# A gated mix of linear attention and a GeGLU feed-forward: tile 0's key sums ahead of the q folds, an up result copied by another engine, and other banks for the q folds

## The chip, the cores and the metric

The kernel runs on one core of one Trainium2 chip. The metric is the device time of one execution in microseconds (us). The core has a matrix engine (TensorE, PE in the profile; its weight loads are shown apart as PEld), a vector engine (VectorE, DVE), an engine for activations (ScalarE, ACT), GpSimd (POOL) and SyncE (SP), which here only issues DMAs. Each engine works through its own queue in order and waits on semaphores that other engines raise. TensorE writes its results into PSUM, which the kernel uses as eight banks of 512 float32 columns, numbered 0 to 7. A bank has to be emptied by VectorE or ScalarE before TensorE may write it again.

## What is computed

```python
# x: 2048 tokens x 640; 32 heads of 20; feed-forward width 1728
g = sigmoid((x * gate_w).sum(-1, keepdims=True))
q, k, v = split(x @ wqkv)                      # each 2048 x 32 x 20
pq, pk = q @ w_phi[h], k @ w_phi[h]            # per head, 20 x 20
phi_q = concat(softmax(pq), softmax(-pq))      # 40 features per head
phi_k = concat(softmax(pk), softmax(-pk))
kv  = sum_s phi_k[s] (outer) v[s];  z = sum_s phi_k[s]
a = ((phi_q @ kv) / (phi_q @ z + 1e-6)) @ wo
b = (gelu_tanh(x @ w_gate) * (x @ w_up)) @ w_down
out = g * a + (1 - g) * b
```

## The kernel before

The 2048 tokens are 16 tiles of 128 (the feed-forward works on 4 blocks of 512). `attention_state` writes out by hand the order in which work is issued to the engines, and a small scheduler (`_Sched`) turns each read and write of a buffer or a bank into semaphore waits. There is no planner: what a line issues goes to the end of its engine's queue.

Four steps matter here.

**Folding.** The per-head 20 x 20 matrix is multiplied into the key weights and the query weights ahead of the tiles: `fold("k", ...)` and `fold("q", ...)`, 55 small matmuls each (L400). The results fill five banks with a row block each (the `main` list, one bank for each of the five blocks `kt` = 0 to 4) and two banks with the remaining heads (the `tail` list). The softmax does not change when one of its 20 columns is subtracted from the others, so only 19 columns are kept: `fold_evac` copies the reference column (L426 on ScalarE, L428 on VectorE for block 0) and subtracts it on VectorE (L429). Block 3 goes another way: `fold_stage` copies the whole bank to SBUF on ScalarE (L438), and GpSimd subtracts (L442). `evacs` is the order in which VectorE empties the banks. A "strip" in that list (L449) is a memset of 19 columns of the second bank of a pair, which pads the last group of three heads.

**Key, value and query tiles.** `k_tile`, `v_tile` and `q_tile` take a pair of banks (b, b+1) and run ten matmuls of some 304 to 345 columns (L452), five for each bank. ScalarE then takes two exponentials from the pair (L523), for tiles 0 to 3 and 5 a small gate exponential as well (L513), or copies the values (L493). A query tile's exponentials leave through a DMA transpose on SP (L561). `k_norm(t)` is `k_sums(t)` (a VectorE sum over each head's features, L574) and `k_scale(t)` (a reciprocal, L582, and a multiplication, L583). `gram(t)` multiplies the normalised keys with the values (L594). The loop over the 16 tiles issues 12 more key tiles, the query tiles, 7 value tiles and 12 grams.

**Up results ahead of time.** `up_ahead(j, b, ek)` computes one chunk of `x @ w_up` for the first 512 tokens into bank b and copies it to SBUF, on VectorE (L538) or ScalarE (L541). Chunks 4, 5 and 6 are made early (`upf`), chunks 2 and 3 late (`upl`), just before the q folds. The feed-forward then runs only the gate half of these chunks for block 0.

**Feed-forward.** `gateups(0)` runs the chunks in the order 0, 1, 13, 2, 3, and so on, on the bank pairs (0,1) and (6,7) in turn. Chunk 13 is half as wide: one bank, a half-height gelu (L728) and two half products on VectorE (L733). Other chunks have a gelu (L720) and one product (L722). The last four grams are issued behind chunks 0, 1, 13 and 2. Chunk 3 writes bank 0, which chunk 13 used.

The order written out around the change is:

```python
v(6, 2); v(7, 4); k(0, 6)
up_ahead(3, ...); up_ahead(4, ...)
fold("q", ...)
k(1, 2); k(2, 4); k(3, 0); v(8, 6)
k_norm(0); k_norm(1); k_norm(2); k_norm(3)
for s in range(16): ...
```

Of the kernel before, what the change touches and what calls it, by code (L numbers as in the profile page):

```python
# [3 lines left out]
P = 128  # L4
BF16 = mybir.dt.bfloat16
F32 = mybir.dt.float32
AF = mybir.ActivationFunctionType
# [100 lines left out]
class _Kernel:  # L108
# [269 lines left out]
        i = s // 2  # L378
        return kt, i, (a - self.HLO[i]) * self.DH, c * self.DH, (z - a + 1) * self.DH

    def fold(self, name, main, tail, evacs):

        sc = self.sc
        wT, wkey = (self.wkT, "wkT") if name == "k" else (self.wqT, "wqT")
        M = lambda r, kt: (main[kt], [self.fold_item(r, kt, s, False) for s in range(r, 8, 2)])
        T = lambda r, j: (tail[j], [self.fold_item(r, kt, s, True) for kt in ((0, 1, 2), (3, 4))[j]
                                    for s in ((8,), (7, 9))[r]])
        halves = ([M(0, 0), M(0, 1), M(0, 2), T(0, 1), M(0, 3), M(0, 4), T(0, 0)],
                  [M(1, 3), M(1, 4), T(1, 0), M(1, 0), M(1, 1), M(1, 2), T(1, 1)])
        order = []  # L390
        for r, runs in enumerate(halves):
            at = 0
            for b, items in runs:
                for x, it in enumerate(items):
                    order.append((at, r, b, x == 0, x == len(items) - 1, it))
                    at += it[-1]
        opener = {}
        for _, r, b, top, bot, (kt, i, k0, c, n) in sorted(order, key=lambda o: o[:2]):
            a, opens = 64 * r, opener.setdefault(b, r) == r
            sc.op("pe", lambda e: e.matmul(  # L400
                self.bank(b)[:, c:c + n], wT[a:a + 64, i, kt * P:(kt + 1) * P],
                self.BD[a:a + 64, i, k0:k0 + n], start=opens and top, stop=bot and not opens, skip_group_check=True),
                reads=[wkey, ("BD", i)], writes=[("ps", b)] + ([("turn", b)] if bot else []), signal=bot,
                after=[("turn", b)] if top and not opens else ())
        self.fold_stage(name, 3, main[3])
        for what, x in evacs:
            if what == "strip":
                self.strip(x)
            elif what == "tail":
                self.fold_evac(name, (0, 3)[x], (3, 2)[x], tail[x], self.HM, self.H)  # L410
            else:
                self.fold_evac(name, x, 1, main[x], 0, self.HM)
# [30 lines left out]
            dst, src[:, :, 0:self.E], src[:, :, self.E].unsqueeze(2).to_broadcast([P, self.HM, self.E]), ALU.subtract),  # L443
            reads=[key], writes=[("w%s2" % name, kt)])

    def strip(self, b):

        c = (b + 1) * 512 + 304
        self.sc.op("dve", lambda e: e.memset(self.ps[:, c:c + self.E], 0.0), writes=[("ps", b + 1)])  # L449

    def mm(self, bank, c0, n, lhs, rhs, first, fin, reads):
        self.sc.op("pe", lambda e: e.matmul(  # L452
# [174 lines left out]
    def attention_state(self):  # L627
        NT = self.NT
        sc = self.sc
        ones = self.nc.const_aps.tensor(1.0, [P, 512], BF16)  # L630
        for n in (512, 512, 512, 512, 512, 512, 128, 128, 128):
            sc.op("pe", lambda e: e.matmul(self.bank(0, n), ones[:, 0:P], ones[:, 0:n], start=True, stop=True),  # L632
                  writes=[("ps", 0)])
        vs, ve, xt = self.v_step, self.v_first_evac, self.x_transpose
        xt(0, "d")
        xt(1, "a")
        for i in range(3):
            for a, b in ((0, 2), (64, 3)):
                sc.op("pe", lambda e: e.matmul(self.bank(b, P), ones[a:a + 64, 0:P], ones[a:a + 64, 0:P], start=True,
                                               stop=True), writes=[("ps", b)])  # L640
        xt(2, "d")
        xt(3, "a")
        for kt in range(4):
            for t in range(4):
                vs(t, kt)
        self.blockdiag()
        self.gate_column(6)
        for t in range(4):
            vs(t, 4)
            ve([t], "ad"[t % 2], False)  # L650
            if t == 2:
                ve([0, 1, 2], "a", True)
        ve([3], "d", True)
        v, k, q = self.v_tile, self.k_tile, self.q_tile
        self.up_ahead(0, 7, "d")
        self.up_ahead(1, 6, "a")
        self.up_ahead(2, 4, "d")
        v(4, 2)
        self.v_split(5, 0)
        m, t, p = "main", "tail", "strip"  # L660
        self.fold("k", (3, 4, 6, 5, 7), (0, 1), [(m, 0), (m, 1), (m, 2), (m, 4), (p, 6), (t, 0), (t, 1)])
        v(6, 2)
        v(7, 4)
        k(0, 6)
        self.up_ahead(3, 3, "d")
        self.up_ahead(4, 2, "a")
        self.fold("q", (3, 4, 5, 0, 1), (6, 7), [(m, 0), (p, 2), (m, 1), (m, 2), (p, 4), (m, 4), (p, 0), (t, 0), (t, 1),
                                               (p, 6)])
        k(1, 2)
        k(2, 4)  # L670
        k(3, 0)
        v(8, 6)
        self.k_norm(0)
        for t in range(1, 4):
            self.k_norm(t)
        nk, nv, ng = 4, 9, 0
        pieces = self.gate_pieces()
        for s in range(NT):
            r = s % 4
            if r != 1:  # L680
                k(nk, 2)
                self.k_norm(nk)
                nk += 1
            if s and r != 0:
                self.gram(ng)
                ng += 1
            if s and r in (0, 1):
                v(nv, 0)
                nv += 1
            q(s, 6)  # L690
            if s:
                pieces.pop(0)()
        for p in pieces:
            p()
        self.down_weights()
# [244 lines left out]
```

## Time and profile before

| | |
|---|---|
| Median of 3 runs | 284.63 us (284.04 to 284.73) |
| The profiled execution's own time | 284.38 us |
| Its span, first to last instruction | 283.1 us |
| Granted TensorE clock | 1.000 |
| PE busy | 278.9 us (98%) |
| PEld busy | 173.5 us (61%) |
| DVE busy | 173.7 us (61%) |
| ACT busy | 106.8 us (38%) |
| POOL busy | 15.1 us (5%) |

The profile is of one execution. "Busy" is the union of an engine's instructions on the time axis. A matmul's row runs from its start to its modelled end, and the next one starts before that end, so what TensorE loses is read from the starts of successive groups and not from its busy share. A bracket such as [0.30 <-DVE ps L449] behind a row gives the idle time of the engine just before that instruction and what ended it, as it is inferred from semaphore events.

### The profile page before, as it was taken

The numbers are of one execution on the slowest core, as the hardware profiler recorded it, in microseconds if no ns is written. First come the engines' busy times: TensorE is split into PE (matmuls) and PEld (weight loads), VectorE is DVE, ScalarE is ACT, GpSimd is POOL, SyncE is SP. The second block draws the span as 40 slices with busy tenths as digits, with TensorE's granted clock in tenths as the row PEclk, the third lists the DMA queues.
The fourth block names the chain that finished last, engine by engine and source line by source line (L and its number), as shares of the span: only waits on it lengthen the run. The fifth ranks groups of instructions, "written<-read, shape, count | busy, mean of one in ns | idle before, by whom it ended". The sixth has DMA issues, their size and how long they took to land.

```text
span 283.1 us, 6982 instructions
## 1 busy us (share of the span) xinstructions
PE 278.9 (98%) x2958; PEld 173.5 (61%) x2972; DVE 173.7 (61%) x329; ACT 106.8 (38%) x201; POOL 15.1 (5%) x69
## 2 busy tenths in 40 slices
PE   8999999999999999999999999999999999999996
PEld 4566777777765444444444444445777777777786
DVE  1365999999999523667243324225883883883801
ACT  4246987878783423223232223221112112112011
POOL 7511010101100000000000000000000000000000
DMA  7999079888799920011000000000152152242221
GB/s 229 211 214 187 4 132 151 165 162 162 147 187 244 347 81 2 0 23 27 0 0 0 2 0 0 2 0 0 25 77 63 53 63 60 71 52 68 73 72 49
DMA packets 60234, 24.11 MB, mean 85 GB/s; under 512 B 50986, under 2 KB 59690, under 8 KB 60202
## 3 DMA queue, kind: packets, MB, share of 16 engines
q1 hardware_dynamic: 59536, 23.63, 39.5%
q8 instruction: 23, 0.38, 0.6%
q10 hardware_dynamic: 666, 0.03, 0.2%
q14 instruction: 9, 0.07, 0.1%
HBM read 9.04 MB, written 2.62 MB: 41 GB/s over the span
## 4 chain that ended last, share of the span: by engine, by line
PE 76%; DVE 13%; issue 9%; ACT 0%; DVEq 0%; ACTq 0%
PE ps L452 41%; PE ps L804 29%; DVE Dk L574 9%; DVE Dk L582 3%; PE ps L464 2%; PE ps L749 2%; PE ps L632 1%; PE ps L400 1%; DVE wq L429 0%; PE ps L341 0%; DVE hT L722 0%; DVE Ek L583 0%; ACT gl L720 0%; DVE hT L733 0%; ACT outsb L817 0%
## 5 line engine op out<-in xcount | busy, mean ns | idle before, releaser
L452 PE MATMUL ps<-xT,wu_sb 128*128 128x512 bf16 x255 | 63.0, 379 | 0.4
L452 PE MATMUL ps<-xT,wg_sb 128*128 128x512 bf16 x251 | 62.0, 379 | 0.9 <-ACT gl L720 0.3
L720 ACT ACTIVATE gl<-ps 128x512 bf16<-128x512 f32 x52 | 31.0, 597 | 71.0 <-PE ps L452 68.0
L804 PE MATMUL ps<-wd_sb,hT 64*128 64x320 bf16 x648 | 48.4, 296 | 0.0
L722 DVE TENSOR_TENSOR hT<-ps,gl 128x512 bf16<-128x512 f32 x34 | 23.2, 690 | 37.7 <-PE ps L452 37.7
L452 PEld LDWEIGHTS ps<-xT,wu_sb 128*128 128x128 bf16 x260 | 25.4, 98 | 30.4
L452 PEld LDWEIGHTS ps<-xT,wg_sb 128*128 128x128 bf16 x260 | 25.0, 98 | 29.8 <-issue 0.6
L817 ACT ACTIVATE outsb<-ps,Gm 128x320 bf16<-128x320 f32 (+2 forms) x31 | 14.5, 515 | 71.8 <-PE ps L804 71.8
L452 PE MATMUL ps<-w,xT 128*128 128x304 bf16 (+5 forms) x280 | 40.3, 296 | 0.0
L804 PEld LDWEIGHTS ps<-wd_sb,hT 64*128 64x128 bf16 x648 | 30.9, 94 | 12.2 <-issue 0.4
L452 PEld LDWEIGHTS ps<-w,xT 128*128 128x128 bf16 x280 | 26.2, 97 | 10.8 <-DVE ps L449 0.3
L804 PE MATMUL ps<-wo_sb,goT 64*128 64x320 bf16 (+2 forms) x340 | 26.5, 288 | 0.0
L583 DVE TENSOR_TENSOR Ek<-Ek,Dk 128x1320 bf16<-128x1320 bf16 x16 | 24.5, 1533 | 0.5
L775 DVE TENSOR_TENSOR O<-ps,RH 128x640 bf16<-128x640 f32 x32 | 24.8, 815 | 0.0
L574 DVE TENSOR_REDUCE Dk<-Ek 128x66 f32<-128x1320 bf16 x16 | 24.3, 1519 | 0.1
L452 PE MATMUL ps<-wq,xT 128*128 128x304 bf16 x160 | 23.3, 292 | 0.0
L523 ACT ACTIVATE Eqt<-ps 128x627 bf16<-128x627 f32 x32 | 20.5, 693 | 6.4 <-PE ps L452 6.4
L523 ACT ACTIVATE Ek<-ps 128x627 bf16<-128x627 f32 x32 | 20.5, 693 | 2.3 <-PE ps L452 2.0
L722 DVE TENSOR_TENSOR xT<-ps,gl 128x512 bf16<-128x512 f32 x13 | 9.0, 692 | 18.2 <-PE ps L452 18.2
L804 PEld LDWEIGHTS ps<-wo_sb,goT 64*128 64x128 bf16 x340 | 15.9, 94 | 5.3
L452 PEld LDWEIGHTS ps<-wq,xT 128*128 128x128 bf16 x160 | 15.0, 97 | 4.5
L804 PE MATMUL ps<-wd_sb,xT 64*128 64x320 bf16 (+2 forms) x270 | 16.0, 269 | 0.0
(89 smaller groups left out, 186.0 us busy)
## 6 DMA issues: line engine op xcount, KB each, us to landing
out_dram<-outsb SPq DMA_DIRECT2D x7, 320.0 KB, 2.4
wd_sb<-in_B_w_down_dram SPq DMA_DIRECT2D x1, 2080.0 KB, 10.2
wg_sb<-in_B_w_gate_dram SPq DMA_DIRECT2D x5, 224.0 KB, 3.6
wg_sb<-in_B_w_gate_dram SPq DMA_DIRECT2D x5, 192.0 KB, 3.7
wu_sb<-in_B_w_up_dram SPq DMA_DIRECT2D x5, 192.0 KB, 5.0
w<-in_A_wqkv_dram SPq DMA_DIRECT2D x5, 160.0 KB, 3.9
wo_sb<-in_A_wo_dram SPq DMA_DIRECT2D x1, 800.0 KB, 9.7
xtok<-in_A_x_dram SPq DMA_DIRECT2D x2, 320.0 KB, 3.1
```

Of the source, the lines that this page charges most:

```text
L452: self.sc.op("pe", lambda e: e.matmul(self.ps[:, bank * 512 + c0:bank * 512 + c0 + n], lhs, rhs, start=first, stop=fin), reads=reads, writ ...
L464: sc.op("pe", lambda e, c0=c0, n=n, bk=bk, col=col: e.matmul(self.bank(bk)[:, col:col + n], self.xT[:, kt, t * P:(t + 1) * P], self.w3[:, ...
L523: self.sc.op("act", lambda e: e.activation(dst, src, AF.Exp, scale=scale), reads=[("ps", b), ("ps", b + 1)], writes=[(name, sl, s)])
L574: self.sc.op("dve", lambda e: e.tensor_reduce(self.Dk[:, se, 0, :].rearrange("p (u h) -> p u h", h=self.HG), self.k_view(se), AX.X, ALU.ad ...
L582: sc.op("dve", lambda e: e.reciprocal(R, D), reads=[("Dk", se)], writes=[("Rk", se)])
L583: sc.op("dve", lambda e: e.tensor_tensor(v, v, R.rearrange("p (u h) -> p u h", h=self.HG).unsqueeze(3).to_broadcast([P, 2 * self.G, self.H ...
L720: sc.op("act", lambda e: e.activation(self.gl[:, slot, :], self.bank(banks[0]), AF.Gelu_apprx_tanh), reads=[("ps", banks[0])], writes=[("g ...
L722: sc.op("dve", lambda e: e.tensor_tensor(hT, up, self.gl[:, slot, :], ALU.mult), reads=[upk, ("gl", slot)], writes=[("hT", hk, c)], guard=old)
L749: sc.op("pe", lambda e: e.matmul(self.ps[:, o:o + n], self.Eq[a:a + 64, g, t * P:(t + 1) * P], self.KV[a:a + 64, g, 0:n], start=(g in (0, ...
L775: dve(lambda e, o=o, f=f, s=s: e.tensor_tensor(o, V[s][:, :, 0:DH], f, ALU.mult), rb + [key(6 + s)], [("O", s, sl)], guard=old)
L804: sc.op("pe", lambda e: e.matmul(self.bank(bk, w), lhs, rhs, start=opens and x == 0, stop=end and not opens, skip_group_check=True), reads ...
L817: sc.op("act", lambda e: e.activation(dst, self.bank(bk, w), AF.Copy, scale=g), reads=rd, writes=wr)
```

## The change

```diff
-    def fold(self, name, main, tail, evacs):
+    def fold(self, name, main, tail, evacs, clear=None):
...
         self.fold_stage(name, 3, main[3])
+        if clear is not None:
+            self.strip(clear, "a")
         for what, x in evacs:
...
-    def strip(self, b):
+    def strip(self, b, ek="d"):
         c = (b + 1) * 512 + 304
-        self.sc.op("dve", lambda e: e.memset(self.ps[:, c:c + self.E], 0.0), writes=[("ps", b + 1)])
+        dst, wr = self.ps[:, c:c + self.E], [("ps", b + 1)]
+        if ek == "d":
+            self.sc.op("dve", lambda e: e.memset(dst, 0.0), writes=wr)
+        else:
+            zero = self.nc.const_aps.tensor(0.0, [P, self.E], F32)
+            self.sc.op("act", lambda e: e.activation(dst, zero, AF.Copy), writes=wr)
...
-        self.up_ahead(3, 3, "d")
+        self.up_ahead(3, 0, "a")
         self.up_ahead(4, 2, "a")
-        self.fold("q", (3, 4, 5, 0, 1), (6, 7), [(m, 0), (p, 2), (m, 1), (m, 2), (p, 4), (m, 4), (p, 0), (t, 0), (t, 1),
-                                               (p, 6)])
+        self.k_sums(0)
+        self.fold("q", (4, 5, 0, 3, 1), (6, 7), [(m, 0), (m, 1), (p, 4), (m, 2), (m, 4), (p, 0), (t, 0), (t, 1), (p, 6)],
+                  2)
         k(1, 2)
         k(2, 4)
         k(3, 0)
         v(8, 6)
-        self.k_norm(0)
+        self.k_scale(0)
         for t in range(1, 4):
             self.k_norm(t)
```

The late up result of chunk 2 goes to bank 0 instead of bank 3, and ScalarE copies it out instead of VectorE. VectorE's sum for key tile 0 is issued ahead of the q folds' evacuation instead of behind it. The row blocks 0 to 4 of the q fold go to banks 4, 5, 0, 3, 1 instead of 3, 4, 5, 0, 1, so the block that ScalarE stages now lies in bank 3. The strip of bank 3 is written by ScalarE, right behind that staging, instead of by a VectorE memset behind block 0. TensorE's instructions are the same in number and order, and only banks differ. No DMA is added, removed or moved.

## The prediction

> **What bounds the kernel now.** I read the chain of waits first, then the windows, then the timeline around the two places that the change touches. In the chain (start, length, work) VectorE's key sums seem to hold everything from 29.6 to 87.3 us:
>
> ```profile
> 29.61 1.51 DVE Dk L574
> 31.15 0.58 DVE Dk L582
> ...
> 87.27 0.96 DVE hT L722 x2
> 88.58 0.44 DVE hT L733
> 89.02 0.59 ACT gl L720
> 89.62 7.50 PE ps L452 x34
> ```
>
> The windows qualify that (columns: length; busy PE, PEld, DVE, ACT, POOL, each with its count; clock; DMA share; GB/s):
>
> ```profile
> 25.90:32.67 6.77, 6.77 (x54) 4.66 (x51) 6.42 (x13) 5.53 (x17) 0.98 (x1) 1.00 0.39 85
> 32.67:81.29 48.62, 48.62 (x474) 36.88 (x472) 47.73 (x41) 39.98 (x69) 4.31 (x11) 1.00 0.81 148
> 81.29:89.62 8.33, 7.90 (x75) 4.36 (x75) 7.98 (x10) 4.94 (x7) 0.00 (x0) 1.00 1.02 229
> ```
>
> In the long middle VectorE is busy for 47.73 of 48.62 us, but so is TensorE, and the clock is full. What TensorE loses has to be counted from starts. In the timeline a query or key tile takes 1.29 us from its start to the next group's (35.67 to 36.96), a value tile 1.36 (34.31 to 35.67), a gram 0.35 (33.96 to 34.31), ten 512-column matmuls 2.15 (83.81 to 85.96), five of them 1.07 (86.31 to 87.38).
>
> - 25.90 to 32.67: four key tiles and one value tile, 4 x 1.29 + 1.36 = 6.52 of 6.77. Lost: about 0.25.
> - 32.67 to 81.29: 16 query tiles, 11 key tiles, 7 value tiles, 12 grams: 27 x 1.29 + 7 x 1.36 + 12 x 0.35 = 48.55 of 48.62. Lost: under 0.1.
> - 81.29 to 89.62: 2 x 2.15 + 2 x 1.07 + 4 x 0.35 = 7.84 of 8.33. Lost: 0.49, nearly all behind the last gram, which starts at 88.80 and should hand over at 89.15; chunk 3 starts at 89.62, 0.47 late.
>
> So TensorE bounds the kernel, and VectorE's backlog reaches it at two spots only. The first, in the timeline (start, length, engine, line, operation, idle time before):
>
> ```profile
> 23.84 0.69 DVE L538 COPY upl<-ps 128x512 f32<-128x512 f32 x1 [1.96 <-PE ps L452]
> 23.98 0.18 ACT L513 ACTIVATE gcol<-ps 128x1 f32<-128x1 f32 x1
> 24.91 0.60 ACT L541 ACTIVATE upl<-ps 128x512 f32<-128x512 f32 x1 [0.76 <-PE ps L452]
> 25.62 0.18 DVE L428 COPY wref<-ps 128x25 f32<-128x25 f32 x1 [1.09 <-PE ps L400]
> 25.69 0.59 ACT L438 ACTIVATE qstage<-ps 128x500 f32<-128x500 f32 x1 [0.18 <-PE ps L400]
> 26.57 0.07 DVE L449 MEMSET ps<- 128x19 f32 x1
> 26.70 0.37 PEld L452 LDWEIGHTS ps<-w,xT 128*128 128x128 bf16 x4 [0.30 <-DVE ps L449]
> 29.61 1.50 DVE L574 TENSOR_REDUCE Dk<-Ek 128x66 f32<-128x1320 bf16 x1
> ```
>
> Tile 1's keys start at 25.90 in bank 2; their second half is due at 25.90 + 0.65 = 26.55 but starts at 26.70, when VectorE's strip has cleared bank 3. The second spot, with a later chunk 13 as the undisturbed case below the dots:
>
> ```profile
> 87.58 0.59 ACT L728 ACTIVATE gl<-ps 64x512 bf16<-64x512 f32 x1 [1.90 <-PE ps L452]
> 88.58 0.89 DVE L733 TENSOR_TENSOR hT<-ps,gl 64x256 bf16<-64x256 f32 x2
> 89.59 4.01 PEld L452 LDWEIGHTS ps<-xT,wg_sb 128*128 128x128 bf16 x20 [0.41 <-issue]
> ...
> 112.48 0.59 ACT L728 ACTIVATE gl<-ps 64x512 bf16<-64x512 f32 x1 [1.56 <-PE ps L452]
> 113.17 0.89 DVE L733 TENSOR_TENSOR hT<-ps,gl 64x256 bf16<-64x256 f32 x2 [1.08 <-ACT gl L728]
> ```
>
> Chunk 3 needs bank 0, whose last readers are chunk 13's two products. They start 1.00 us after their gelu's start here and 0.69 later on, because VectorE is behind. They end at 88.58 + 0.89 = 89.47, and chunk 3 loads its weights 0.12 later. After 89.62 TensorE goes on to the end, so what it gains by then stays gained.
>
> **The change part by part.**
>
> *The up copy.* VectorE loses a 0.69 us copy, ScalarE gains one of 0.60 (its row at 24.91). ScalarE is free after its gate exponential at 24.16, so the copy lies at 24.16 to 24.76, in the 0.76 us that it idled; the second copy stays at 24.91. The fold reaches bank 0 in its third run, a quarter or so into 1.08 us that begin at 24.81: about 25.1. The cover is 0.3 us; without it each further microsecond delays the fold. Cost: nothing.
>
> *The sums of tile 0.* Their input is ready at 24.10 (exponentials at 22.82 plus 1.28). VectorE, which idled from the end of its copy at 24.53 to 25.62, runs 1.50 us from about 24.17 to 25.67. Behind it in the queue stands the whole evacuation of the fold, which starts at 25.70 instead of 25.62: 0.08 late. Five q evacuations feed banks 4, 5, 0, 1, 6 and 7 to the key and value tiles that TensorE issues next.
>
> *Strip and banks.* One 0.07 memset leaves VectorE. The ScalarE strip has no row: the gate exponential (0.17 to 0.18, one column) and the reference copies (five, median 0.21) bound it at 0.17 to 0.21. It waits for the staging copy of the same bank, which ends at 25.69 + 0.59 = 26.28; so it ends at 26.50 to 26.55, and TensorE's second half starts at 26.55 to 26.60 instead of 26.70. The reference copies behind it slip some 0.2, so block 1's subtraction starts at about 26.68 instead of at the end of block 0's (26.58), 0.1 late. Then, at 0.65 a block and 0.45 a tail: bank 4 free at 26.6 (due 27.2), bank 5 at 27.4 (due 27.85), bank 0 at 28.05 (due 28.5), bank 1 at 28.8 (due 29.15), bank 6 at 29.25 (due 29.8). Smallest slack 0.35. Gain of TensorE here: s = 0.12, between 0 (a strip as late as VectorE's) and 0.25 (all that is lost in this stretch).
>
> One rule speaks against this part. The Trainium skill ("ScalarE: Activation LUTs", section "Rules for kernel authors") sends plain arithmetic to VectorE, and budgets about 0.3 us an ACTIVATE plus 0.83 ns an element; by it the strip would take an estimated 0.32 us, end at 26.65 and make s nothing. The one-column row at 0.18 says otherwise.
>
> *VectorE from there.* The evacuation ends at 29.7 and the sums are already done, so tile 1's sums start near 31.85 instead of 33.20. 1.35 us ahead (1.2 to 1.5), VectorE keeps that lead: its inputs are ready, closest for tile 14 (exponentials done at 78.27, sums at 80.06 before, 78.7 after). It ends the keys at 86.0 instead of 87.3.
>
> *The second spot.* Chunk 0's and 1's products then end at 87.3, before chunk 13's gelu does. The gelu starts at 87.58 - s; the products follow as in the later row, 0.69 + 0.89 = 1.58, and TensorE 0.12 + 0.03 behind them: 89.31 - s instead of 89.62. Gain 0.31 beside s; with the 0.05 step between a gate exponential's end at 39.85 and the weight load at 39.90, 0.38; at most 0.47, when TensorE is held by nothing; none, if the wait is another.
>
> The rest of VectorE's 1.35 us goes into idle time before chunk 13's products. A second rule would value it more: the Trainium skill ("Perfetto Trace Analysis", "Identifying the Most-Contended Engine") takes the engine with the highest occupancy as the one to speed up and distrusts TensorE's busy share. By occupancy the middle stretch is VectorE's, and the gain would be the whole 1.35 us. The count from starts leaves 0.1 us there.
>
> Sum: 0.12 + 0.31 = 0.43, with the shorter step 0.5; I take 0.45. The profiled execution has 284.38 us, 283.1 of span and 1.3 around it, which the change does not touch: 283.9. It lies 0.25 below the median; on the median's scale 284.63 - 0.45 = **284.2**.
>
> **The rivals.**
>
> *A: the chain is right, VectorE's whole lead arrives.* For it: 98% busy and an unbroken chain to 87 us. Against it: TensorE has only 0.8 us to win in all three stretches. 284.63 - 1.35 = 283.3.
>
> *B: the wait at 89.6 stays.* For it: the chain names chunk 2's gelu, ending at 89.61, as what released chunk 3. Against it: that gelu reads bank 6. Only s remains: 284.5.
>
> *C: slower, the sums are not hidden.* Place: VectorE's queue at 24.2. If the sums run only when the fold's results are there (25.62), the evacuation is 1.5 late, tile 3's keys in bank 1 are late by 1.5 - 0.35 = 1.15, and VectorE's lead is gone. TensorE, that much later, no longer stalls 0.47 at the second spot: +0.7, 285.3. It decides from about 0.8 us of lateness (0.35 slack and 0.45 of gain). Against it: the input is ready 1.5 us before the fold's first result.
>
> **How the numbers follow.** Forecast 0.60, A 0.13, B 0.17, C 0.10. The forecast's own range is 283.8 to 284.6 (gains from 0 to 0.8). The three runs before spread over 0.7 us, so medians of three may move by some 0.3; down to A and toward C this makes 283.3 to 284.9. A measurement of this kernel tells about 0.3% (0.85 us) from no change. Faster by more: most of A and a tenth of the forecast, 0.19. Slower by more: half of C and a little scatter, 0.07. Within: 0.74.
>
> **What would show it.** Right: sums of tile 0 at 24.2; no stall before tile 1's second half; chunk 13's products 0.7 us after their gelu's start; chunk 3 at 89.1 to 89.3; VectorE idle before these products. Wrong: chunk 3 still at 89.5 (B), or before 88.7 (A), or weight loads in 27 to 31 us that wait for VectorE (C). A strip well above 0.2 us would take s away. Any new wait behind 90 us would make the whole sum wrong.

## The result and the profile after

| | before | changed |
|---|---|---|
| Median | 284.41 us (22 runs, 284.04 to 284.83) | 283.96 us (22 runs, 283.50 to 284.46) |
| Ratio | | 0.9983, 95% interval 0.9976 to 0.9989 |
| Profiled execution, time and span | 284.38 and 283.1 us | 284.17 and 282.9 us |
| DVE busy, instructions | 173.7 us, 329 | 172.8 us, 327 |
| ACT busy, instructions | 106.8 us, 201 | 107.5 us, 203 |

The change makes the kernel 0.45 us faster by the medians (0.3 to 0.7 by the interval of the ratio). That is clear of scatter, and under the 0.3% that the prediction took for no change. With 22 runs instead of 3 the median of the kernel before came out at 284.41, 0.22 lower.

The rows of the kernel before from which the distances below are counted and which the prediction does not show, in its timeline (start, length, engine, line, operation, idle time before and what ended it):

```profile
24.81 1.16 PE L400 MATMUL ps<-BD,wqT 64*128 64x80 bf16 x55
32.67 1.46 PE L452 MATMUL ps<-wq,xT 128*128 128x304 bf16 x10
33.20 1.52 DVE L574 TENSOR_REDUCE Dk<-Ek 128x66 f32<-128x1320 bf16 x1
...
88.80 0.49 PE L594 MATMUL ps<-vaug,Ek 128*128 128x63 bf16 x11
89.62 2.10 PE L452 MATMUL ps<-xT,wg_sb 128*128 128x512 bf16 x9 [0.32 <-ACT gl L720]
```

L400 has the same number in both kernels; behind the edits the numbers are 2 to 8 higher (L452 is L459, L449 is L453 and, for ScalarE, L456, L733 is L741). The experiments shift them by a line or two more.

The first spot, in the timeline of the changed kernel:

```profile
24.47 1.53 DVE L581 TENSOR_REDUCE Dk<-Ek 128x66 f32<-128x1320 bf16 x1 [2.30 <-ACT gcol L520]
25.09 1.16 PE L400 MATMUL ps<-BD,wqT 64*128 64x80 bf16 x55
...
25.91 0.18 DVE L430 COPY wref<-ps 128x25 f32<-128x25 f32 x1
25.98 0.59 ACT L440 ACTIVATE qstage<-ps 128x500 f32<-128x500 f32 x1 [0.18 <-PE ps L400]
...
26.59 0.19 ACT L456 ACTIVATE ps<-const-float32-0.0 128x19 f32<-128x19 f32 x1
...
26.84 5.77 PEld L459 LDWEIGHTS ps<-w,xT 128*128 128x128 bf16 x45 [0.15 <-ACT ps L456]
27.00 0.65 DVE L431 TENSOR_TENSOR wq<-ps,wref 128x475 bf16<-128x475 f32 x1 [0.22 <-ACT wref L428]
...
32.09 1.52 DVE L581 TENSOR_REDUCE Dk<-Ek 128x66 f32<-128x1320 bf16 x1
```

Here the q fold starts at 25.09, in the kernel before at 24.81. Over the profiles of this study its start lies between 24.49 and 25.28, whatever the kernel: in this execution TensorE waited 0.38 us, until 5.80, for a weight transfer, long before the change. So starts are compared from the fold's first matmul on. The sums of tile 0 run in VectorE's idle time. The first reference copy follows 0.82 after the fold's start (0.81 before), so they delay nothing. The weight load for tile 1's second half comes 1.75 after the fold's start (26.84 - 25.09) instead of 1.89 (26.70 - 24.81), with 0.15 idle before it instead of 0.30. And the sums of tile 1 start at 32.09 - 25.09 = 7.00 instead of 33.20 - 24.81 = 8.39: VectorE's lead is 1.39 us.

The second spot, in the timeline of the changed kernel:

```profile
86.16 1.28 DVE L730 TENSOR_TENSOR hT<-ps,gl 128x512 bf16<-128x512 f32 x2
...
87.68 0.59 ACT L736 ACTIVATE gl<-ps 64x512 bf16<-64x512 f32 x1 [1.90 <-PE ps L459]
...
88.37 0.89 DVE L741 TENSOR_TENSOR hT<-ps,gl 64x256 bf16<-64x256 f32 x2 [0.93 <-ACT gl L736]
...
88.89 0.50 PE L601 MATMUL ps<-vaug,Ek 128*128 128x63 bf16 x11
89.09 0.60 ACT L728 ACTIVATE gl<-ps 128x512 bf16<-128x512 f32 x1 [0.83 <-PE ps L459]
89.37 4.01 PEld L459 LDWEIGHTS ps<-xT,wg_sb 128*128 128x128 bf16 x20
```

VectorE is through with chunks 0 and 1 at 87.44 and idles 0.93 us until chunk 13's gelu ends. The products start 0.69 after that gelu's start (1.00 before) and end at 89.26, and chunk 3's weights load 0.11 later. The last gram starts at 88.89 and should hand over 0.35 later, at 89.24. Chunk 3's first matmul is at 89.40: 0.16 lost instead of 0.47. Chunk 2's gelu, which the chain of before named as the releaser, now ends at 89.69, after chunk 3 has begun.

The chain of waits (start, length, work) no longer passes through VectorE anywhere. That is not proof that TensorE waits for nothing: chunk 3 is still 0.16 us late, and run e4 shows that bank 0 is the cause.

```profile
89.06 0.33 PE ps L601 x11
89.39 0.01 issue
89.40 27.14 PE ps L459 x125
```

The window of the second spot (length; busy PE, PEld, DVE, ACT, POOL, each with its count; clock; DMA share; GB/s) has TensorE busy for 8.32 of 8.33 us, against 7.90 before, and VectorE for 6.93 against 7.98. It is the same stretch of the clock and not of the work, and takes in four matmuls more (79 instead of 75); the 0.16 us don't show in it, so the gain is read from the starts:

```profile
81.29:89.62 8.33, 8.32 (x79) 4.53 (x77) 6.93 (x8) 4.88 (x8) 0.00 (x0) 1.00 1.01 225
```

### The profile page after: what moved, and what is told of

It reads as the page before. It is cut to its first block, busy times and chain, and to the rows that moved or that the text cites. A ratio compares the mean times of both kernels' runs of the same rounds, so it can differ in the third digit from the quotient of the medians.

```text
span 282.9 us, 6996 instructions
## 1 busy us (share of the span) xinstructions
PE 279.4 (99%) x2972; PEld 173.5 (61%) x2972; DVE 172.8 (61%) x327; ACT 107.5 (38%) x203; POOL 15.2 (5%) x69
## 4 chain that ended last, share of the span: by engine, by line
PE 97%; DMA 1%; SPq 0%; issue 0%; ACT 0%
PE ps L459 62%; PE ps L812 29%; PE ps L757 2%; PE ps L471 2%; PE ps L601 2%; DMA w<-in_A_wqkv_dram 1%; PE ps L400 1%; SPq L230 0%; ACT outsb L825 0%; PE ps L366 0%
## 5 line engine op out<-in xcount | busy, mean ns | idle before, releaser
L459 PE MATMUL ps<-xT,wu_sb 128*128 128x512 bf16 x260 | 64.1, 379 | 0.0
L459 PE MATMUL ps<-xT,wg_sb 128*128 128x512 bf16 x260 | 64.0, 379 | 0.0
L459 PEld LDWEIGHTS ps<-xT,wu_sb 128*128 128x128 bf16 x260 | 25.4, 98 | 30.4
L459 PEld LDWEIGHTS ps<-xT,wg_sb 128*128 128x128 bf16 x260 | 25.0, 98 | 29.5 <-issue 0.2
L459 PE MATMUL ps<-w,xT 128*128 128x304 bf16 (+5 forms) x280 | 40.2, 296 | 0.0
L459 PEld LDWEIGHTS ps<-w,xT 128*128 128x128 bf16 x280 | 26.3, 97 | 10.5 <-ACT gcol L520 0.2
L459 PE MATMUL ps<-wq,xT 128*128 128x304 bf16 x160 | 23.2, 292 | 0.0
L459 PEld LDWEIGHTS ps<-wq,xT 128*128 128x128 bf16 x160 | 15.0, 98 | 4.5
```

What stands on the lines that cost most here:

```text
L459: self.sc.op("pe", lambda e: e.matmul(self.ps[:, bank * 512 + c0:bank * 512 + c0 + n], lhs, rhs, start=first, stop=fin), reads=reads, writ ...
```

## The experiments

All are followed by the same three distances in the profiled execution: from the fold's first matmul to the first query tile (which holds the first spot), on to chunk 3's first matmul ("the stretch"), and the idle time behind the last gram (chunk 3's start minus the last gram's, minus 0.35). The last column is the profiled time less the fold's start and the stretch. The ratio of an experiment is to runs of the kernel before that were taken beside it; their medians were 284.45 us (e1 to e4), 284.62 (e5 to e8) and 284.47 (e9 and e10), so medians of different groups are not to be compared more closely than some 0.2 us.

| | to first query tile | stretch | idle behind last gram | median us | ratio to before, 95% | rest |
|---|---|---|---|---|---|---|
| before | 7.86 | 64.81 | 0.47 | 284.41 | | 194.76 |
| changed | 7.68 | 64.31 | 0.16 | 283.96 | 0.9983 (0.9976 to 0.9989) | 194.77 |
| e1_sums_only | 8.11 | 64.75 | 0.16 | 284.28 | 0.9997 (0.9988 to 1.0006) | 194.80 |
| e2_sums_back | 7.67 | 64.99 | 0.84 | 284.56 | 1.0008 (0.9999 to 1.0018) | 194.76 |
| e3_before_bank1 | 7.86 | 64.34 | 0.00 | 283.95 | 0.9980 (0.9971 to 0.9988) | 194.76 |
| e4_after_bank1 | 7.68 | 64.15 | -0.01 | 283.83 | 0.9970 (0.9954 to 0.9985) | 194.76 |
| e5_load_half | 7.67 | 64.30 | 0.16 | 283.90 | 0.9976 (0.9966 to 0.9986) | 194.85 |
| e6_load_full | 7.67 | 64.98 | 0.84 | 284.52 | 1.0000 (0.9990 to 1.0010) | 194.76 |
| e7_norm_ahead | 9.29 | 65.92 | 0.15 | 285.42 | 1.0028 (1.0016 to 1.0040) | 194.78 |
| e8_strip_dve | 7.75 | 64.37 | 0.15 | 283.83 | 0.9977 (0.9966 to 0.9988) | 194.78 |
| e9_back_strip_dve | 7.75 | 64.73 | 0.51 | 284.33 | 0.9997 (0.9988 to 1.0006) | 194.77 |
| e10_bank1_strip_dve | 7.75 | 64.21 | -0.01 | 283.83 | 0.9974 (0.9963 to 0.9984) | 194.81 |

The rest is 194.76 to 194.85 us in all twelve kernels. So what any of them wins or loses lies in the stretch, apart from the scatter of the start, and after chunk 3's start nothing above 0.1 us is given back or gained. Each stretch is read in one execution. How well such a reading repeats is seen at the first query tile: the kernel before and e3 both have 7.86, the five with the new banks, a ScalarE strip and an evacuation on time have 7.67 or 7.68, and the three with the new banks and a VectorE strip 7.75. That is far finer than the medians tell.

**e1_sums_only: the sums ahead, and nothing else of the change.**

```diff
         self.up_ahead(4, 2, "a")
+        self.k_sums(0)
         self.fold("q", (3, 4, 5, 0, 1), ...)
...
-        self.k_norm(0)
+        self.k_scale(0)
```

> Kernel before with one edit: tile 0's sums ahead of the q folds; banks, strip and up copy stay. I follow the stretch from the first q fold matmul to chunk 3's first matmul: 64.81 us before, 64.31 after. Theory (TensorE bounds; VectorE counts only where a bank is late): the sums now start behind VectorE's up copy and end some 0.4 us after the fold's first result, so the strip of bank 3 and with it tile 1's second half slip by 0.4, tiles 1 to 3 with them; at the second spot chunk 3 is then held by the chain behind chunk 13's gelu: stretch 64.9, time 284.5, although VectorE ends the keys about 1 us earlier against the fold's start. Rival A (VectorE's lead is what counts): stretch 63.8, time 283.4.

The stretch is 64.75. VectorE wins 1.30 us (chunk 0's product 61.16 after the fold's start instead of 62.46), and the idle time at the second spot falls to the 0.16 of the changed kernel. But the first spot loses 0.25: the sums start at once behind the up copy, end 1.15 us after the fold's start, and the strip of bank 3, with it tile 1's second half, slips. The loss is 0.25, not the expected 0.4, because VectorE's sums start 0.08 us before the copy's row ends and the evacuation before theirs. The two effects almost cancel, and rival A is off by 0.95 us.

**e2_sums_back: the other banks, the ScalarE strip and the ScalarE up copy, without the sums ahead.**

```diff
-        self.k_sums(0)
         self.fold("q", (4, 5, 0, 3, 1), ..., 2)
...
-        self.k_scale(0)
+        self.k_norm(0)
```

> Changed kernel with tile 0's sums put back behind the fold; banks, ScalarE strip and ScalarE up copy stay. Theory (two gains that need each other): tile 1's keys still start their second half on time (0.15 to 0.18 us won), but VectorE ends the keys as late as before, so chunk 13's products hold chunk 3 longer: the idle time behind the last gram grows from 0.47 to about 0.65 and eats the early gain. Stretch 64.7 to 64.8, time 284.35 (no change from the kernel before). Rival (the gains simply add): stretch 64.63, time 284.2. Rival B (the second spot is not VectorE's): idle behind the last gram stays at 0.16 as in the changed kernel, time 284.0.

The early gain is there in full (7.67), and all of it is eaten: 0.84 us idle behind the last gram. The stretch is even 0.18 longer than before, against an expected gain of up to 0.1. VectorE's rows say why:

```profile
25.78 0.66 DVE L431 TENSOR_TENSOR wq<-ps,wref 128x475 bf16<-128x475 f32 x1
26.65 0.66 DVE L431 TENSOR_TENSOR wq<-ps,wref 128x475 bf16<-128x475 f32 x1 [0.22 <-ACT wref L428]
...
29.73 1.50 DVE L581 TENSOR_REDUCE Dk<-Ek 128x66 f32<-128x1320 bf16 x1
```

VectorE idles 0.22 us between block 0 and block 1, until ScalarE's reference copy is there, and its sums start 4.98 after the fold's start instead of 4.80. Run e9 takes this up.

**e3_before_bank1 and e4_after_bank1: chunk 3 of block 0 in bank 1.** Bank 1 held chunk 0's up half, and is read out well before.

```diff
             done = early and b == 0
+            if done and c == 3:
+                banks = (banks[1], banks[0])
```

> Kernel before with one edit: chunk 3 of block 0 writes bank 1 (empty since chunk 0's product) instead of bank 0 (chunk 13's). Theory: the 0.47 us behind the last gram is the wait for chunk 13's two products in bank 0; it falls to nothing, stretch 64.34, time 283.95, as good as the whole change, with VectorE as late as before. Rival B (the wait is chunk 2's gelu, as the chain names it): stretch stays 64.8, time 284.4.

> Changed kernel with chunk 3 of block 0 in bank 1. Theory: the 0.16 us that are left behind the last gram go too: stretch 64.15, time 283.8, the lowest of all. Rival B: no change, 64.31 and 283.96.

Both came out as the theory had them. In the kernel before with this edit, VectorE is as late as ever and its products end after chunk 3 has begun, in the timeline:

```profile
88.29 0.89 DVE L735 TENSOR_TENSOR hT<-ps,gl 64x256 bf16<-64x256 f32 x2
88.48 0.49 PE L594 MATMUL ps<-vaug,Ek 128*128 128x63 bf16 x11
88.69 0.60 ACT L722 ACTIVATE gl<-ps 128x512 bf16<-128x512 f32 x1 [0.83 <-PE ps L452]
88.80 2.71 PEld L452 LDWEIGHTS ps<-xT,wg_sb 128*128 128x128 bf16 x14
```

Products end at 89.18, chunk 2's gelu at 89.29, and chunk 3 loads its weights at 88.80. So the 0.47 us were bank 0's, and an edit of two lines takes them all away without moving any work: 283.95 us, the time of the whole change. On top of the change it takes the last 0.16.

**e5_load_half and e6_load_full: extra VectorE work behind the last key tile**, of half a tile's sum and of a whole one; its result is not used.

```diff
+        sc.op("dve", lambda e: e.tensor_reduce(
+            self.scratch[:, 0:33].rearrange("p (u h) -> p u h", h=self.HG), self.k_view(0)[:, 0:11], AX.X, ALU.add),
+            reads=[("Ek", 0, 0), ("Ek", 0, 1), ("Ekc", 0)], writes=["scratch"])
         for p in pieces:
             p()
```

> Changed kernel with an extra VectorE sum of half a key tile into an unused buffer, behind tile 15's scaling (about 0.8 us; result not used). Theory: VectorE idles 0.93 us before chunk 13's products, so the extra work fits: stretch 64.31 unchanged, products still 0.69 behind their gelu's start, time as the changed kernel. Rival A (VectorE's end sets the time): stretch 65.1, +0.8.

> Changed kernel with an extra VectorE sum of a whole key tile in the same place (about 1.55 us; result not used). Theory: 0.93 of it is covered, the rest delays chunk 13's products and chunk 3: stretch 64.31 + 0.6 = 64.9, time +0.6, about that of the kernel before. Rival A: stretch 65.85, +1.5.

The half sum took 0.84 us and cost nothing (64.30): chunk 13's products start 0.69 us after their gelu, as without it, in the timeline of e5:

```profile
85.91 0.84 DVE L702 TENSOR_REDUCE scratch<-Ek 128x33 f32<-128x660 bf16 x1
...
87.29 0.59 ACT L740 ACTIVATE gl<-ps 64x512 bf16<-64x512 f32 x1 [1.90 <-PE ps L460]
87.98 0.88 DVE L745 TENSOR_TENSOR hT<-ps,gl 64x256 bf16<-64x256 f32 x2
```

The whole one took 1.53 and cost 0.67, in the timeline of e6:

```profile
85.85 1.53 DVE L702 TENSOR_REDUCE scratch<-Ek 128x66 f32<-128x1320 bf16 x1
...
87.23 0.59 ACT L740 ACTIVATE gl<-ps 64x512 bf16<-64x512 f32 x1 [1.90 <-PE ps L460]
87.29 1.28 DVE L734 TENSOR_TENSOR hT<-ps,gl 128x512 bf16<-128x512 f32 x2
...
88.60 0.89 DVE L745 TENSOR_TENSOR hT<-ps,gl 64x256 bf16<-64x256 f32 x2
...
89.64 2.10 PE L460 MATMUL ps<-xT,wg_sb 128*128 128x512 bf16 x9 [0.69 <-DVE hT L745]
```

With VectorE 1.5 us later the whole gain is gone; with 0.84 it is untouched. Some 0.9 us of VectorE's 1.39 are idle time in the changed kernel.

**e7_norm_ahead: too much ahead of the fold.** All of tile 0's normalisation, not the sums alone.

```diff
-        self.k_sums(0)
+        self.k_norm(0)
         self.fold("q", (4, 5, 0, 3, 1), ..., 2)
...
-        self.k_scale(0)
```

> Changed kernel with the whole of tile 0's normalisation (sums, reciprocal, scaling: 3.6 us) ahead of the q folds instead of the sums alone. Theory, as in rival C of the prediction: the fold's evacuations start 2.1 us late; with some 0.35 us of slack the keys of tile 3 in bank 1 and what follows are late by 1.7 to 1.8, partly regained where TensorE then waits for nothing at the second spot (0.16): stretch 64.31 + 1.6 = 65.9, time 285.5 (1.1 above the kernel before). VectorE's total work is the same. Rival A (only VectorE's end counts): VectorE ends as early as in the changed kernel, time 284.0.

The stretch is 65.92, the time 285.42, and rival A's 284.0 is out. The first evacuation starts 27.68 - 24.69 = 2.99 after the fold's start, 2.17 late. In the timeline the key tiles queue up behind it:

```profile
26.43 0.51 PEld L459 LDWEIGHTS ps<-w,xT 128*128 128x128 bf16 x5 [0.15 <-ACT ps L456]
...
28.59 0.50 PEld L459 LDWEIGHTS ps<-w,xT 128*128 128x128 bf16 x5 [1.66 <-DVE wq L431]
...
29.31 0.51 PEld L459 LDWEIGHTS ps<-w,xT 128*128 128x128 bf16 x5 [0.21 <-DVE ps L453]
```

The place was wrong: tile 2's keys in bank 4 wait first and longest, then their second half in bank 5, and no weight load of tile 3 waits for VectorE. The sum came out by luck, since two errors cancel. At the first query tile the lateness is 9.29 - 7.68 = 1.61 instead of 1.7 to 1.8, so 2.17 - 1.61 = 0.56 us of slack covered the rest and not 0.35. And the 0.16 us at the second spot are not regained (0.15 remain), because the gelu and the products behind it move with TensorE.

**e8_strip_dve, e9_back_strip_dve and e10_bank1_strip_dve: the strip of bank 3 by VectorE**, in the changed kernel, in e2 and in e4.

```diff
-        self.fold("q", (4, 5, 0, 3, 1), (6, 7), [(m, 0), (m, 1), (p, 4), (m, 2), (m, 4), (p, 0), (t, 0), (t, 1), (p, 6)],
-                  2)
+        self.fold("q", (4, 5, 0, 3, 1), (6, 7), [(m, 0), (p, 2), (m, 1), (p, 4), (m, 2), (m, 4), (p, 0), (t, 0), (t, 1), (p, 6)])
```

> Changed kernel with the strip of bank 3 written by VectorE behind block 0's evacuation, as before, instead of by ScalarE. Theory: tile 1's second half starts some 0.15 us later, chunk 3 with it: stretch 64.45, time 284.1. Rival (the other banks alone do it, the strip's engine does not matter, since VectorE's strip ends at the same 0.9 us behind the fold's results): stretch 64.3, time 283.96.

> Changed kernel with tile 0's sums back behind the fold, and the strip of bank 3 by VectorE: of the change only the other banks and the ScalarE up copy are left. The earlier run with the sums back had 64.99 us for the stretch, 0.18 above the kernel before, and VectorE idle for 0.22 us before block 1's subtraction, until ScalarE's reference copy. Theory (that idle time is the ScalarE strip's doing, and VectorE's end alone sets chunk 3 when the sums are behind): the idle time is gone, the sums of tile 0 start 4.8 us after the fold's start as in the kernel before, stretch 64.75 to 64.8, time 284.4. Rival (the new order of banks delays VectorE): sums again at 4.98, stretch 64.99, time 284.55.

> Changed kernel with chunk 3 of block 0 in bank 1 and the strip of bank 3 by VectorE. Theory (with bank 1 nothing holds TensorE at the second spot, so the early stretch decides alone, and the ScalarE strip is worth 0.07 there): stretch 64.22 against 64.15 with the ScalarE strip, time 283.85, not to be told from it. Rival (VectorE's 0.2 us earlier end is worth something later): 64.22, but the time at or below 283.6.

In e8 the stretch lies between the two expectations (64.37): the strip's engine is worth 0.07 us on TensorE, and the new banks alone bring the other 0.11 of the early 0.18. VectorE's strip is itself 0.07 earlier than before (1.69 after the fold's start instead of 1.76), which fits that bank 3 is no longer the bank that VectorE's preceding subtraction reads. VectorE's rows of e9 next to those of e2 settle e2:

```profile
26.30 1.30 DVE L431 TENSOR_TENSOR wq<-ps,wref 128x475 bf16<-128x475 f32 x2
26.97 0.79 DVE L453 MEMSET ps<- 128x19 f32 x2
...
30.02 1.50 DVE L581 TENSOR_REDUCE Dk<-Ek 128x66 f32<-128x1320 bf16 x1
```

Blocks 0 and 1 run without a gap, the sums start 4.74 after the fold's start, and the stretch is 64.73. So the ScalarE strip costs VectorE 0.24 us, by holding up ScalarE's reference copies behind it. In the changed kernel that cost falls into VectorE's idle time. e10, where TensorE waits for VectorE at neither spot, has the stretch of the theory (64.21 for 64.22). Its time can't be told from e4's or e8's: all three have the lowest median, 283.83, although e8's stretch is 0.06 longer than the changed kernel's. That e4 and e10 beat the changed one is shown by the stretch (0.16 and 0.10 less) and not by the medians or the intervals, which overlap.

## Why the prediction was right

The time on record, 284.2, lies 0.24 above the measured 283.96, because it stood on a base of 284.63; with the base of 284.41 the gain of 0.45 comes out as forecast. Point by point:

- **TensorE bounds the kernel.** Shown. VectorE's work ahead changed the time only through two banks: e3 takes the later wait away with VectorE as late as before, and e5 gives VectorE 0.84 us more for nothing. Rival A (283.3) would need the whole lead to arrive; the chain's unbroken VectorE rows were a chain of one engine following itself.
- **First spot, s = 0.12 (0 to 0.25).** Measured 0.18. The strip took 0.19 us (bounds 0.17 to 0.21), and the weight load came 0.14 earlier, at the early end of what was worked out. The other 0.04 is with the tiles behind it. The prediction counted 0.25 us lost in this stretch, 0.15 of it at tile 1, but gave the rest no gain. It fits tile 2's keys: in the kernel before their weights load at 27.38, 0.12 behind block 1's subtraction in the same bank, and in the changed kernel they follow tile 1's without a gap. In e8 it stays (0.11 = 0.07 of earlier strip + 0.04). No run takes it apart from the strip.
- **The up copy costs nothing.** Right: ScalarE's copy ran from 24.31 to 24.93, 0.16 us before the fold's first matmul, and the second copy followed 0.11 after that matmul (0.10 before).
- **The sums cost nothing.** Right: 0.01 late instead of 0.08. That the cover can run out is shown by e7.
- **The reference copies slip by 0.2 and block 1 by 0.1.** Block 1 starts 1.91 after the fold's start instead of 1.80. Against a VectorE strip on the same banks it is more, 0.24 over the whole evacuation (e2 against e9).
- **VectorE's lead, 1.35.** Measured 1.39.
- **Second spot, 0.31 beside s.** Measured 0.47 - 0.16 = 0.31, with the step of 0.69 from gelu to products and 0.11 from products to weight load.
- **The sum.** 0.18 + 0.31 = 0.49, and 0.50 read directly from the stretch (64.81 to 64.31), where 0.43 was worked out and 0.45 taken.
- **Rival B (the wait is chunk 2's gelu).** Out by e3: chunk 3 starts while that gelu runs.
- **Rival C (late evacuations).** It did not come: the evacuation was 0.01 us late. Forced in e7, it struck at bank 4 and not at bank 1. Its +0.7 was too high: it took 0.35 us of slack where e7 shows 0.56, and left the early gain out. From the runs, an evacuation 1.5 us late would cost an estimated 1.5 - 0.56 - 0.18 - 0.31 = 0.45 us over the kernel before, where 0.18 is the early gain and 0.31 what the second spot gives back.
- **The two rules of the Trainium skill.** "ScalarE: Activation LUTs" ("Rules for kernel authors") gives its 0.3 us for an ACTIVATE whose bias is a pointer operand; the prediction left that condition out, and the strip is issued without a bias. By that row the strip would have taken an estimated 0.32 us; it took 0.19, so s did not vanish. The advice itself, plain arithmetic to VectorE, would have cost little here: 0.06 us in the stretch, and no difference in time that can be told (e8). "Perfetto Trace Analysis" ("Identifying the Most-Contended Engine") would have picked VectorE as the engine to speed up, and the prediction read its lead at the full 1.35 from that; the runs gave 0.31 for it at the second spot.

What made e2's expectation miss was a step outside the prediction: that the idle time at the second spot would grow by the early gain alone. The strip's cost to VectorE had to be added. The two halves of the change are not a sum of two gains: the banks alone bring nothing measurable (e9, 0.08 in the stretch, e2 below zero), the sums alone 0.06 (e1), both together 0.50.

## What to carry to other kernels

An engine that is 98% busy and on the chain need not be the bound when another one is as busy: count from the starts of successive groups what the matrix engine really loses, and price an edit by that. Where a late engine holds one bank, look first whether the waiting work can use a bank that is already empty; here that edit of two lines was worth as much as moving the work. An early gain can be eaten by the next wait downstream (e2, e9), so measure both spots from a common start, and don't judge such a change by its halves alone.

## What the runs showed of the hardware

- The start of one execution scatters more than the change is worth: the q fold began between 24.49 and 25.28 us in twelve profiles of kernels whose work up to there hardly differs. From chunk 3 on they agree within 0.1 us in 195.
- In the changed kernel a VectorE instruction that waits for nothing of the one ahead started before that one's row ended (the reference copy 0.09 us before the sums' end, at 25.91 against 26.00); a memset that the program makes wait for the preceding subtraction of the same bank started 0.07 us later than one without that wait (1.76 after the fold's start before, 1.69 in e8).
- ScalarE overlaps in the same way: in the kernel before its reference copies began 0.11 us before the staging copy's end (26.17 against 26.28). In the changed kernel the strip, which waits for that copy, began 0.02 after its end (26.59 against 26.57), and the copies began 0.13 behind the strip's start. So in these rows a wait on the engine's own preceding instruction cost the overlap as well as the strip's length.
